# Attention and a two-layer network on one core: the second weights loaded ahead of two attention pairs, the second batch's pairs spread over more steps, and the leaky ReLU of twelve steps summed on GpSimd

## Chip, cores and metric

One Trainium2 chip, one core used. The metric is the device time of one execution in microseconds (us); several executions are made and their median is compared. The engines are TensorE (PE: matmuls; PEld: its weight loads), VectorE (DVE), ScalarE (ACT), GpSimd (POOL) and SyncE (SP), which issues the transfers (DMA).

## What is computed

q, k and v are 8 batches x 8 heads x 576 positions x 64, float32. Each head gets two attentions: a softmax over the sequence averaged down by 4 (144 positions), its result repeated 4 times, and a softmax over a band of |i - j| < 4. Their sum, laid out as 4608 tokens x 512, goes through two layers with a leaky ReLU between them. The layers' weights arrive as float64.

```
q_d, k_d, v_d = (a.reshape(B, H, 144, 4, 64).mean(axis=3) for a in (q, k, v))
out_up    = repeat(softmax(scale * q_d @ k_d.T) @ v_d, 4)
out_local = softmax(where(abs(i - j) < 4, scale * q @ k.T, -1e9)) @ v
x = (out_up + out_local) -> [4608, 512]
h = x @ w_in                                       # [4608, 2048]
g = maximum(h, 0.0) + alpha * minimum(h, 0.0)      # alpha: one per column of h
out = g @ w_out                                    # [4608, 512]
```

## The kernel before

**The stream.** The 4608 tokens are cut into 18 chunks of 256, the 2048 hidden columns into 8 pairs of 128; a *step* is one chunk and one pair, 144 steps in all, step 0 to 7 being the first chunk. Each float32 operand is split into an upper part (rounded to the type that TensorE multiplies at full speed) and a lower part, and each product is made of three: upper x upper, upper x lower, lower x upper. A step is: `hidden` (24 matmuls, L752, into PSUM tile h), `slopes` (ScalarE writes slope*h to tile t in SBUF and sign*h over h in PSUM, two halves each, L760 and L761), `larger` (VectorE takes the maximum of the two into t, L764), `split` (ScalarE rounds t to gh, L769; GpSimd subtracts, gl = t - gh, by the helper at L69) and `product` (24 matmuls, L798, into o). The sign belongs to the columns with alpha over 1; it is multiplied into the second layer's weights, so that a maximum serves for all.

**Weights.** Each pair's weights of w_in and w_out come as raw float64 (1 MB each, `load_raw`), as pairs of 32-bit words, and are turned into float32 parts by `make`: `magnitude` (ScalarE, L184, tile temp), `reach` (VectorE, L188 and L189), `bits` (VectorE, L193 and L194), `upper` (ScalarE: wih L199, or two halves of woh times sign, L203) and `lower` (VectorE: wil L207, or two halves of wol, L211). wih0, wil0 hold pairs 0 and 1, wih1 pairs 2 and 3, and so on. The first five pairs (`N_EARLY`) are decoded ahead of the stream, 128 x 1024 at a time; the last three beside steps 0 to 6 or so, by halves of 128 x 512, with their temporaries in PSUM (`bank`).

**The first batch** is computed ahead of the stream (`first_batch`), pair of heads by pair of heads: transfers of q, k (tile fqk) and v (fv), the averaging (L453, L455, L471, L473), scores, exponentials, the sums fxs (L512), and their split into xh (ScalarE, L518) and xl (VectorE, L519), the operands of hidden. The table `ORDER` lists in which order the one load queue (SyncE's) is given the transfers: `i0`..`i2` and `o0`..`o2` are raw weights of w_in and w_out of pair 0 to 2, `a0`..`a3` q, k and v of the four pairs of heads, `b0`..`b3` the windows of the local attention. For what stands before the stream the order on the other engines is left to a scheduler, which follows the priorities and the loads.

**The other batches** come in pieces beside the stream. For the averaged attention of pair hp of batch b, `down` makes: six loads (ld, L232), each with two folds on GpSimd (the helper `add`, L72; results s2q, s2k, s2v), `flip` (TensorE transposes, L250, tile qkT), `operands` (ScalarE copies qd and kd, L255 and L258), `scores` (TensorE, L263, tile s), `peak` (VectorE, L267), `exps` (ScalarE, L273 and L275, tile dp), `invert`, `scale` (ScalarE, L282), `turn` (TensorE transposes, L287, tile pT), `turned` (ScalarE copies, L291, tile th), `weigh` (TensorE, L297, tile pv) and `store`. The local attention of the later batches follows in units that begin at the times of the table `UNITS` and then every 5.92 steps.

**What sets the order.** From the stream on, all is written into a list of events, each with a time in *steps*; the program issues them sorted by it, and each engine executes its own in that order. hidden(s) stands at s - 1.95, slopes at s - 1.45, larger at s - 1.15, split at s - 1.0, product at s + 0.6. For `down`, the loads and folds begin at t0 (`FIRST[hp]` for batch 1), 0.4 steps apart, and the pieces behind them follow at t1 + pace * lag with the lags

```
(0, flip), (0.5, operands), (1.0, scores), (1.6, peak), (1.7, exps), (2.3, invert),
(2.4, scale), (3.0, turn, 0), (3.01, turn, 1), (3.4, turned, 0), (3.41, turned, 1),
(4.0, weigh), (4.5, store)
```

and t1 = t0 + 6 * gap + 0.3 (t1 = t0 for the first, whose folds are done in the start). pace is 0.75 for the four pairs of batch 1, 1.0 for all others. Pieces of batch 1 thus stand between steps 0 and 13.

## Time and profile before

| | us |
|---|---|
| median of 3 runs | 1014.43 |
| lowest to highest | 1014.23 to 1015.88 |
| the profiled execution's own time | 1012.62 |
| its span in the trace | 1010.8 |
| TensorE busy | 960.6 |
| VectorE busy | 832.8 |
| ScalarE busy | 560.2 |
| GpSimd busy | 482.1 |

The span goes from the first to the last instruction in the trace; the execution's own time has 1.8 us more around it. Busy time counts instructions in execution, not waits. The profile comes from one execution, the median from others.

### The profile page before, as it was taken

Reading aid. Unit: us, or ns where it says so; the run is one execution under the profiler, and the core shown is the slowest. Engines: PE = TensorE matmul, PEld = TensorE weight load, DVE = VectorE, ACT = ScalarE, POOL = GpSimd, SP = SyncE. Lnnn points to the kernel's source line nnn. Section 1 sums busy time; section 2 is a strip of 40 time slices with the busy share of each in tenths; the row PEclk is TensorE's granted clock in tenths of the full one; section 3 lists DMA queues with packets and bytes.
Section 4 is the critical chain, followed back from the end, with each engine's and each line's share of the span. In section 5 each row is a group of like instructions: output and inputs, shape, how many; then the busy total and the mean of one; then the engine's idle time right before and its main releaser. Section 6 shows DMA issues by size and latency. Waiting matters only on the chain.

```text
span 1010.8 us, 17864 instructions
## 1 busy us (share of the span) xinstructions
PE 960.6 (95%) x6402; PEld 852.7 (84%) x6402; DVE 832.8 (82%) x1347; ACT 560.2 (55%) x1483; POOL 482.1 (48%) x612
## 2 busy tenths in 40 slices
PE   5877989999999999999999999999999999999998
PEld 4756878898888898988888888888988898989997
DVE  6899988899888899899888898898898899997111
ACT  4767766465565555555455555555555554444442
POOL 2040645677665546555554544656555543323221
PEclk9856989999999999999999999999999999999999
DMA  8946443232422322433322332322331412210000
GB/s 191 222 148 242 123 153 98 83 119 83 145 83 73 118 81 78 121 97 93 103 88 66 100 111 71 125 80 74 123 100 60 131 49 61 86 43 22 1 21 22
DMA packets 61218, 98.26 MB, mean 97 GB/s; under 512 B 21578, under 2 KB 26954, under 8 KB 61130
## 3 DMA queue, kind: packets, MB, share of 16 engines
q1 hardware_dynamic: 60938, 96.87, 32.0%
q8 instruction: 50, 0.82, 0.3%
q10 hardware_dynamic: 192, 0.26, 0.1%
q14 instruction: 38, 0.31, 0.1%
HBM read 87.67 MB, written 9.44 MB: 96 GB/s over the span
## 4 chain that ended last, share of the span: by engine, by line
PE 72%; DVE 15%; ACT 4%; issue 3%; DMA 2%; POOL 2%; SPq 2%; DVEq 0%; ACTq 0%; POOLq 0%
PE o L798 33%; PE h L752 33%; DMA raw<-in_moe_w_out 2%; DVE qk L591 2%; DVE lb L650 2%; PE s L263 2%; DVE t L764 1%; PE pv L297 1%; DVE ls L595 1%; DVE temp L193 1%; DVE pv L647 1%; PE xp L659 1%; PE pT L287 1%; DVE temp L194 1%; DMA ld<-in_q 1%
## 5 line engine op out<-in xcount | busy, mean ns | idle before, releaser
L69 POOL TENSOR_TENSOR gl<-t,gh 128x512 fp32r<-128x512 f32 x144 | 186.5, 1295 | 390.8 <-ACT gh L769 347.4
L760 ACT ACTIVATE t<-h,slope 128x256 f32<-128x256 f32 x288 | 136.3, 473 | 203.0 <-PE h L752 166.2
L764 DVE TENSOR_TENSOR t<-h,t 128x512 f32<-128x512 f32 x144 | 99.0, 687 | 113.2 <-ACT h L761 108.6
L752 PE MATMUL h<-xh,wih 128*128 128x256 f32 x1152 | 190.9, 287 | 0.7 <-ACT xh L518 0.7
L798 PE MATMUL o<-woh,gh 128*128 128x512 f32 x576 | 188.1, 407 | 0.4 <-ACT woh L203 0.4
L752 PE MATMUL h<-xl,wih 128*128 128x256 f32 x1152 | 183.7, 281 | 0.6 <-POOL xl L69 0.6
L752 PE MATMUL h<-xh,wil 128*128 128x256 f32 x1152 | 184.1, 282 | 0.0
L798 PE MATMUL o<-wol,gh 128*128 128x512 f32 x576 | 182.1, 397 | 0.1
L798 PE MATMUL o<-woh,gl 128*128 128x512 f32 x576 | 182.1, 397 | 0.0
L752 PEld LDWEIGHTS h<-xh,wih 128*128 128x128 f32 x1152 | 163.5, 190 | 10.5 <-issue 1.8
L72 POOL TENSOR_TENSOR ld<-ld 72x256 f32<-72x256 f32 x168 | 125.4, 747 | 73.9 <-DMA ld<-in_q 49.4
L752 PEld LDWEIGHTS h<-xl,wih 128*128 128x128 f32 x1152 | 156.9, 190 | 0.8 <-POOL xl L69 0.8
L752 PEld LDWEIGHTS h<-xh,wil 128*128 128x128 f32 x1152 | 157.3, 190 | 0.0
L769 ACT CAST gh<-t 128x512 fp32r<-128x512 f32 x144 | 89.1, 619 | 118.7 <-DVE t L764 68.4
L595 DVE TENSOR_REDUCE ls<-qk 128x12 f32<-128x768 f32 (+1 forms) x126 | 136.4, 1083 | 2.8
L798 PEld LDWEIGHTS o<-woh,gl 128*128 128x128 f32 x576 | 108.6, 189 | 26.4
L798 PEld LDWEIGHTS o<-wol,gh 128*128 128x128 f32 x576 | 108.4, 188 | 26.4 <-DVE wol L211 0.7
L761 ACT ACTIVATE h<-h,sign 128x256 f32<-128x256 f32 x288 | 126.4, 439 | 0.0
L650 DVE TENSOR_TENSOR lb<-lb,pv 128x384 f32<-128x384 f32 x202 | 113.9, 564 | 5.5
L798 PEld LDWEIGHTS o<-woh,gh 128*128 128x128 f32 x576 | 98.3, 189 | 16.3 <-issue 2.2
L647 DVE TENSOR_TENSOR pv<-v,lb 128x1152 f32<-128x1152 f32 x84 | 93.6, 1115 | 2.6
L591 DVE TENSOR_TENSOR qk<-k,qp 128x768 f32<-128x768 f32 (+1 forms) x78 | 84.0, 1077 | 0.0
(148 smaller groups left out, 1111.4 us busy)
## 6 DMA issues: line engine op xcount, KB each, us to landing
k<-in_k SPq DMA_DIRECT2D x41, 384.0 KB
v<-in_v SPq DMA_DIRECT2D x41, 384.0 KB
raw<-in_moe_w_in SPq DMA_DIRECT2D x16, 512.0 KB
raw<-in_moe_w_out SPq DMA_DIRECT2D x16, 512.0 KB
ld<-in_q SPq DMA_DIRECT2D x56, 144.0 KB
ld<-in_k SPq DMA_DIRECT2D x56, 144.0 KB
ld<-in_v SPq DMA_DIRECT2D x56, 144.0 KB
q<-in_q SPq DMA_DIRECT2D x42, 192.0 KB
```

What stands on the lines that cost most here:

```text
L69: nc.gpsimd.tensor_tensor(o, a, b, op=ALU.subtract)
L72: nc.gpsimd.tensor_tensor(o, a, b, op=ALU.add)
L591: nc.vector.tensor_tensor(st["pr"][:, :nd], window(tiles[u, "k"], half, d0, nd), st["qp", half].unsqueeze(1).to_broadcast([128, nd, 2, 192 ...
L595: nc.vector.tensor_reduce(out=st["s"][:, half, d0:d0 + nd, :].rearrange("p a b -> p (a b)"), in_=st["pr"][:, :nd].rearrange("p a h (t d) - ...
L647: nc.vector.tensor_tensor(st["pr"][:, :nd], window4(tiles[u, "v"], half, d0, nd), prob(half, d0, nd), op=ALU.mult)
L650: nc.vector.tensor_tensor(st["acc"], st["acc"], st["pr"][:, i], op=ALU.add)
L752: nc.tensor.matmul(ph[:, j], w[:, m, 128 * o:128 * o + 128], x[:, m, :], start=(i == 0), stop=(i == 11))
L760: nc.scalar.activation(t[:, j], hs[st][:, j], AF.Copy, scale=slope[:, f:f + 1])
L761: nc.scalar.activation(hs[st][:, j], hs[st][:, j], AF.Copy, scale=sign[:, f:f + 1])
L764: nc.vector.tensor_tensor(gs[st], hs.pop(st), gs[st], op=ALU.max)
L769: nc.scalar.copy(gh, t)
L798: nc.tensor.matmul(outs[c][m], g[:, j, 128 * m:128 * m + 128], wo[w][n][:, o, :], start=(f == 0 and i == 0), stop=(f == NF - 1 and i == 2))
```

## The change

Four edits. `ORDER` moves i1 and o1 (the second raw weights) ahead of a2 and a3 respectively, with i2 ahead of b3. `down` runs batch 1's pairs at pace 1.0, and `FIRST` begins pair 2 at 2.8 and pair 3 at 5.3 steps. For steps 0 to 11 (`EARLY`) the leaky ReLU is written as a sum: slope*h + relu((sign - slope)*h), in which ScalarE writes the second term to a tile sh in SBUF and GpSimd adds it to t with the helper that does the folds; from step 12 on it stays a maximum on VectorE. One small subtraction makes gain = sign - slope.

```diff
--- before.py
+++ after.py
@@ -37,12 +37,13 @@
 FPT = ('ooo', 'ooo', 'ooo', 'oqo')
 FPV = ('ooo', 'ooo', 'ooo', 'qlq')
 EM = 'bbba'
-ORDER = 'i0 a0 a1 b0 o0 a2 b1 a3 b2 i1 b3 o1 i2'
+ORDER = 'i0 a0 a1 b0 o0 i1 a2 b1 o1 a3 b2 i2 b3'
 N_EARLY = 5
-FIRST = (-1.3, 0.3, 3.0, 5.7)
+FIRST = (-1.3, 0.3, 2.8, 5.3)
 T0_DEC, D_DEC = 0.5, 0.56
 UNITS = {3: 7.5, 4: 12.2, 5: 17.4, 6: 22.7, 7: 28.0}
 U_STEP = 5.92
+EARLY = 12
 BY_HALF = (5, 9, 13, 17, 21)
 FAR = {3: 2, 4: 2, 5: 2, 6: 2}
 
@@ -106,12 +107,14 @@
 
     sign = const.tile([128, NF], F32, name="sign")
     slope = const.tile([128, NF], F32, name="slope")
+    gain = const.tile([128, NF], F32, name="gain")
 
     def load_alpha():
         nc.sync.dma_start(slope, alpha.rearrange("(f p) -> p f", p=128))
         nc.vector.tensor_scalar(sign, slope, 1.0, 2.0, op0=ALU.is_le, op1=ALU.mult)
         nc.vector.tensor_scalar(sign, sign, -1.0, None, op0=ALU.add)
         nc.vector.tensor_tensor(slope, slope, sign, op=ALU.mult)
+        nc.vector.tensor_tensor(gain, sign, slope, op=ALU.subtract)
 
 
     wi, wo = ([[None] * 4, [None] * 4] for _ in range(2))
@@ -755,13 +758,24 @@
 
     def slopes(st):
         t = gs[st] = two.tile([128, 2, T], F32, tag="t", name=f"t{st}")
+        other = hs[st]
+        if st < EARLY:
+            other = late.tile([128, 512], F32, tag="xf", name=f"sh{st}").rearrange("p (j n) -> p j n", j=2)
         for j in range(2):
             f = 2 * (st % NP) + j
             nc.scalar.activation(t[:, j], hs[st][:, j], AF.Copy, scale=slope[:, f:f + 1])
-            nc.scalar.activation(hs[st][:, j], hs[st][:, j], AF.Copy, scale=sign[:, f:f + 1])
+            if st < EARLY:
+                nc.scalar.activation(other[:, j], hs[st][:, j], AF.Relu, scale=gain[:, f:f + 1])
+            else:
+                nc.scalar.activation(other[:, j], hs[st][:, j], AF.Copy, scale=sign[:, f:f + 1])
+        if st < EARLY:
+            hs[st] = other
 
     def larger(st):
-        nc.vector.tensor_tensor(gs[st], hs.pop(st), gs[st], op=ALU.max)
+        if st < EARLY:
+            add(gs[st], hs.pop(st), gs[st])
+        else:
+            nc.vector.tensor_tensor(gs[st], hs.pop(st), gs[st], op=ALU.max)
 
     def split(st):
         t = gs[st]
@@ -854,7 +868,7 @@
         def at(t, f, *args):
             events.append((t, len(events), f, args))
 
-        down(1, 0, FIRST[0], 0.0, 0.75, early=True)
+        down(1, 0, FIRST[0], 0.0, early=True)
     build_masks()
     late = ctx.enter_context(tc.tile_pool(name="late", bufs=1))
 
@@ -884,7 +898,7 @@
         b, hp = 1 + p // 4, p % 4
         if b == 1:
             if hp:
-                down(b, hp, FIRST[hp], 0.4, 0.75)
+                down(b, hp, FIRST[hp], 0.4)
     begin = dict(UNITS)
     for u in range(len(UNITS) + 3, 3 * B + 1):
         begin[u] = begin[u - 1] + U_STEP
```

In the changed kernel the same lines have numbers that are 1 to 14 higher: L72 becomes L73, L69 L70, L188 L191, L287 L290, L519 L522, L752 L755, L798 L812.

**VectorE, the last instructions ahead of the first chunk's last lower operand.** xl0 <- fxs30 belongs to the fourth pair of heads of the first batch; step 0 needs it. raw1_3 is w_out of the fourth pair of weights, raw0_4 w_in of the fifth. Before:

```order
L194 SCALAR_TENSOR_TENSOR temp_791<-raw0_3_847,temp_791 128x1024
L188 TENSOR_SCALAR temp_791<-temp_791 128x1024
L189 TENSOR_SCALAR temp_791<-temp_791 128x1024
L207 TENSOR_TENSOR wil1_830<-temp_791,wih1_829 128x4x256
L512 TENSOR_TENSOR fxs30_770<-fpv30_761,fod3_759 128x256
L193 SCALAR_TENSOR_TENSOR temp_791<-raw1_3_857,temp_791 128x1024
L512 TENSOR_TENSOR rest_89<-fpv38_787,fod3_759 128x64
L188 TENSOR_SCALAR temp_791<-temp_791 128x1024
L519 TENSOR_TENSOR xl0_313<-fxs30_770,xh0_312 128x256
```

With the change:

```order
L196 SCALAR_TENSOR_TENSOR temp_793<-raw1_3_859,temp_793 128x1024
L210 TENSOR_TENSOR wil1_832<-temp_793,wih1_831 128x4x256
L522 TENSOR_TENSOR xl1_330<-fxs24_633,xh1_329 128x256
L197 SCALAR_TENSOR_TENSOR temp_793<-raw1_3_859,temp_793 128x1024
L191 TENSOR_SCALAR temp_793<-temp_793 128x1024
L515 TENSOR_TENSOR fxs30_772<-fpv30_763,fod3_761 128x256
L192 TENSOR_SCALAR temp_793<-temp_793 128x1024
L214 SCALAR_TENSOR_TENSOR wol1_844<-temp_793,sign_78,woh1_843 128x512 x2
L515 TENSOR_TENSOR rest_91<-fpv38_789,fod3_761 128x64
L196 SCALAR_TENSOR_TENSOR temp_793<-raw0_4_871,temp_793 128x1024
L522 TENSOR_TENSOR xl0_315<-fxs30_772,xh0_314 128x256
```

The decoding has moved on ahead of xl0: the bit operations of raw1_3 and its lower parts (wol1) now stand before it, as does the first bit operation of raw0_4; counted from the program's start, two more bit operations of 128x1024, two more of wol's parts and one more scalar operation on temp stand ahead of it.

**GpSimd, from step 0 to the subtraction of step 2.** gl is the lower part of a step's g, t and sh are the two terms of the leaky ReLU, ld1_1 are the loads of the second pair of heads (pair 1) of batch 1 and s2q1_1 its folded q. Before:

```order
L69 TENSOR_TENSOR gl0_1008<-t0_995,gh0_1007 128x512
L69 TENSOR_TENSOR gl1_1066<-t1_1048,gh1_1065 128x512
L72 TENSOR_TENSOR ld1_1_0_1040<-ld1_1_0_1040 72x2x128
L72 TENSOR_TENSOR s2q1_1_1094<-ld1_1_0_1040 72x2x64
L72 TENSOR_TENSOR ld1_1_1_1046<-ld1_1_1_1046 72x2x128
L72 TENSOR_TENSOR s2q1_1_1094<-ld1_1_1_1046 72x2x64
L69 TENSOR_TENSOR gl2_1144<-t2_1107,gh2_1143 128x512
```

With the change:

```order
L73 TENSOR_TENSOR t0_997<-sh0_998,t0_997 128x512
L70 TENSOR_TENSOR gl0_1011<-t0_997,gh0_1010 128x512
L73 TENSOR_TENSOR t1_1047<-sh1_1048,t1_1047 128x512
L70 TENSOR_TENSOR gl1_1061<-t1_1047,gh1_1060 128x512
L73 TENSOR_TENSOR ld1_1_0_1039<-ld1_1_0_1039 72x2x128
L73 TENSOR_TENSOR s2q1_1_1089<-ld1_1_0_1039 72x2x64
L73 TENSOR_TENSOR ld1_1_1_1045<-ld1_1_1_1045 72x2x128
L73 TENSOR_TENSOR s2q1_1_1089<-ld1_1_1_1045 72x2x64
L73 TENSOR_TENSOR t2_1107<-sh2_1108,t2_1107 128x512
L70 TENSOR_TENSOR gl2_1138<-t2_1107,gh2_1137 128x512
```

Each step has an add ahead of its subtraction, and that of step 2 stands behind the folds of the two loads of q.

**TensorE, around hidden of step 7 (h7) and product of step 5 (o0 with gh5, gl5).** pT1_1 is the transposition of pair 1's probabilities dp1_1; qkT1_2 that of pair 2's folded q and k. Before:

```order
L752 MATMUL h7_1489<-xh0_312,wih3_1257 128x256 x4
L752 MATMUL h7_1489<-xh0_312,wil3_1258 128x256 x4
L752 MATMUL h7_1489<-xl0_313,wih3_1257 128x256 x4
L287 MATMUL pT1_1_0_1517<-ident_73,dp1_1_1438 72x96 x3
L287 MATMUL pT1_1_1_1521<-ident_73,dp1_1_1438 72x96 x3
L798 MATMUL o0_0_1112<-woh2_889,gh5_1399 128x512
L798 MATMUL o0_1_1113<-woh2_889,gh5_1399 128x512
```

With the change (the line of dots leaves out the rest of the product, of the same kind):

```order
L755 MATMUL h7_1496<-xl0_315,wih3_1259 128x256 x4
L253 MATMUL qkT1_2_1535<-ident_73,s2q1_2_1303 128x72 x2
L253 MATMUL qkT1_2_1535<-ident_73,s2k1_2_1377 128x72 x2
L812 MATMUL o0_0_1113<-woh2_891,gh5_1403 128x512
L812 MATMUL o0_1_1114<-woh2_891,gh5_1403 128x512
...
L812 MATMUL o0_1_1114<-woh2_891,gl5_1404 128x512
L290 MATMUL pT1_1_0_1577<-ident_73,dp1_1_1477 72x96 x3
L290 MATMUL pT1_1_1_1585<-ident_73,dp1_1_1477 72x96 x3
L755 MATMUL h8_1589<-xh1_329,wih0_81 128x256 x4
```

The transposition pT1_1 has moved from ahead of the product of step 5 to behind it, and the folds' transposition of pair 2 from behind the product to ahead of it.

## Rows read from the trace of the kernel before

**Rows 1.** The page: busy time of each engine, in us, share, instructions.
```profile
PE 960.6 (95%) x6402; PEld 852.7 (84%) x6402; DVE 832.8 (82%) x1347; ACT 560.2 (55%) x1483; POOL 482.1 (48%) x612
```

**Rows 2.** Windows: start:end, length; busy us (instructions) per engine; PEclk; DMA share; GB/s.
```profile
36.00:100.00 64.00, 49.30 (x376) 41.20 (x375) 62.77 (x103) 44.03 (x112) 15.07 (x13) 0.63 0.66 205
100.00:150.00 50.00, 45.38 (x276) 38.38 (x275) 43.15 (x69) 35.54 (x86) 27.55 (x39) 0.93 0.45 137
...
95.00:101.00 6.00, 6.00 (x35) 5.79 (x34) 5.17 (x7) 3.45 (x12) 0.69 (x1) 0.72 0.99 373
```

**Rows 3.** TensorE's timeline: start, duration (us), instructions; in brackets idle time before, releaser.
```profile
85.23 0.58 PE L752 MATMUL h<-xh,wih 128*128 128x256 f32 x1 [0.66 <-ACT xh L518]
...
94.65 1.34 PE L263 MATMUL s<-kd,qd 128*96 128x144 f32 x6 [2.13 <-ACT kd L258]
...
123.13 0.98 PE L263 MATMUL s<-kd,qd 128*96 128x144 f32 x6 [1.28 <-ACT kd L258]
...
134.04 1.14 PE L287 MATMUL pT<-ident,dp 96*72 96x96 f32 x6 [1.52 <-ACT dp L282]
...
141.21 0.34 PE L250 MATMUL qkT<-ident,s2q 72*128 72x72 f32 x2 [1.70 <-ACT th L291]
...
142.25 0.74 PE L752 MATMUL h<-xh,wih 128*128 128x256 f32 x4
...
146.73 0.90 PE L263 MATMUL s<-kd,qd 128*96 128x144 f32 x6
...
161.38 0.32 PE L250 MATMUL qkT<-ident,s2q 72*128 72x72 f32 x2 [0.99 <-POOL gl L69]
...
171.73 0.63 PE L752 MATMUL h<-xh,wih 128*128 128x256 f32 x4
...
174.53 0.63 PE L798 MATMUL o<-woh,gh 128*128 128x512 f32 x2
...
192.50 0.44 PE L659 MATMUL xp<-ident,x 128*128 128x128 f32 x2 [1.72 <-ACT kd L258]
```

**Rows 4.** Window inside the hidden part of step 8, columns as in rows 2.
```profile
144.00:146.00 2.00, 2.00 (x12) 2.00 (x11) 1.97 (x4) 1.25 (x4) 1.92 (x4) 0.50 0.00 0
```

**Rows 5.** VectorE's timeline, columns as in rows 3.
```profile
35.70 0.69 DVE L471 TENSOR_TENSOR fv<-fv 72x512 f32<-72x512 f32 x1 [2.62 <-DMA fv<-in_v]
...
85.81 0.41 DVE L519 TENSOR_TENSOR xl<-fxs,xh 128x256 fp32r<-128x256 f32 x1
86.15 1.22 DVE L194 SCALAR_TENSOR_TENSOR temp<-raw,temp 128x1024 int32<-128x1024 int32 x1
87.29 0.68 DVE L189 TENSOR_SCALAR temp<-temp 128x1024 int32<-128x1024 int32 x1
...
89.36 1.41 DVE L211 SCALAR_TENSOR_TENSOR wol<-temp,sign,woh 128x512 fp32r<-128x512 f32 x2
...
94.49 1.76 DVE L189 TENSOR_SCALAR temp<-temp 128x1024 int32<-128x1024 int32 x1
```

**Rows 6.** ScalarE's timeline.
```profile
99.98 1.32 ACT L203 ACTIVATE woh<-temp,sign 128x512 fp32r<-128x512 f32 x2
...
113.30 0.62 ACT L769 CAST gh<-t 128x512 fp32r<-128x512 f32 x1 [2.76 <-DVE t L764]
```

**Rows 7.** Groups by line: busy us, mean ns, idle before and its main releaser.
```profile
L69 POOL TENSOR_TENSOR gl<-t,gh 128x512 fp32r<-128x512 f32 x144 | 186.5, 1295 | 390.8 <-ACT gh L769 347.4
...
L764 DVE TENSOR_TENSOR t<-h,t 128x512 f32<-128x512 f32 x144 | 99.0, 687 | 113.2 <-ACT h L761 108.6
...
L761 ACT ACTIVATE h<-h,sign 128x256 f32<-128x256 f32 x288 | 126.4, 439 | 0.0
```

**Rows 8.** GpSimd's timeline.
```profile
93.91 1.78 POOL L69 TENSOR_TENSOR gl<-t,gh 128x512 fp32r<-128x512 f32 x1 [31.63 <-ACT gh L769]
...
104.05 0.74 POOL L72 TENSOR_TENSOR ld<-ld 72x256 f32<-72x256 f32 x1 [0.77 <-DMA ld<-in_q]
...
106.64 1.29 POOL L69 TENSOR_TENSOR gl<-t,gh 128x512 fp32r<-128x512 f32 x1
```

## The prediction

> **What bounds the kernel now.** I read the page first. TensorE is busy 95% of the span, VectorE 82%, ScalarE 55%, GpSimd 48% [rows 1]. From about 200 us on TensorE hardly stops, and the change touches nothing there but an offset, so the question is how early the two-layer stream reaches, say, step 12, and what it loses on the way.
>
> The windows come next [rows 2]. From 36 to 100 us VectorE is busy 62.8 of 64 us while TensorE runs at a mean granted clock of 0.63: there VectorE sets the pace. It works off the first batch's attention and the decoding of the weights in one fixed order. From 100 to 150 us VectorE is still busy 43.2 of 50 us and TensorE 45.4, at a clock of 0.93.
>
> Then TensorE's timeline [rows 3]. The first step's matmuls start to run in earnest at 85.23 us. After that TensorE executes a fixed order of steps with small pieces of the second batch's pairs between them, and each time it stops, a piece stands at the head of the queue: 2.13, 1.28, 1.52, 1.70 and 0.99 us, and 1.72 us at 192.50, each waiting for ScalarE or GpSimd, which wait for VectorE or each other. Of the five that end from 94.65 us (first scores) to 161.38 us, ahead of the hidden part of step 12 at 171.73 us, the last four make 5.5 us (the 1.28 us one, of scores too, ends at 123.13 us). Two stretches run at half clock as well: the hidden part of step 8, inside which the granted clock is 0.50, the lower of its two levels (1.2 of 2.4 GHz) [rows 4], takes 146.73 - 142.25 = 4.48 us, where that of step 12 takes 174.53 - 171.73 = 2.80 us [rows 3], so 1.7 us is lost; and the product ahead of it loses about as much (from 134.04 us to 141.21 less the wait of 1.70 are 5.47 us, of which the piece at the front has 1.14 less some 0.2 of overlap: 4.5 us, against 2.8). In all some 8.9 us of the stream can be won back: 5.5 idle and 3.4 at half clock.
>
> **The change, part by part.**
>
> *Loads.* The second weights' two transfers move ahead of the third and fourth pair's q, k, v on the one load queue. For the start this matters through VectorE's order, which the scheduler rewrote with it. I counted what stands ahead of the first chunk's last low operand (xl0 of the fourth pair, at 85.81 us [rows 5]) on VectorE in both programs. The attention work is the same; the changed order has two more of the 1024-wide bit operations, two more 512-wide lower parts and one more 1024-wide scalar operation. Durations from start to next start: 87.29 - 86.15 = 1.14 us; the pair of lower parts 1.32 us, the row's 1.41 less the overlap of some 0.08 that the row before shows (1.22 against 1.14); 0.60 us for the scalar operation, the row's 0.68 less the same [rows 5]. Sum 2 x 1.14 + 1.32 + 0.60 = 4.2 us more work ahead of the stream.
>
> Against that, VectorE waited 2.62 us at 35.70 us for the fourth pair's v [rows 5]. In the changed order 15 more instructions stand ahead of that one, 8 to 9 us of work by the same durations, whereas its data are pushed back by 2 MB. At the window's 205 GB/s 2 MB is 10.2 us; at the 373 GB/s of 95 to 101 us, in which weights land, it is 5.6 [rows 2]. That leaves a wait between 0 and 4.3 us; these 2 MB are weights, so I take the fast end: the wait about vanishes. Handshakes with ScalarE now stand elsewhere (the second weights' magnitude is ahead of the exponentials of pair 1 on ScalarE), and I charge 0.6 us for them. Start: 4.2 - 2.6 + 0.6 = **+2.2 us**. Bounds: +1.6 (wait gone, nothing new) and +6 (wait stays, as much again new).
>
> Behind xl0, ScalarE now has the two signed upper parts of the fifth output weights ahead of the first gh and of the pair's q and k copies, 1.32 us for the two [rows 6], and they wait for VectorE's last bit operation. VectorE needs 6.8 us from the start of xl0 to the end of that (three bit operations, one lower part, two scalar operations and three short ones at the durations above), then ScalarE about 2.7: the first scores start 9.6 us after xl0 instead of 94.65 - 85.81 = 8.8. That is another **+0.8 us**; bounds 0 and +1.5.
>
> *The leaky ReLU.* Twelve max operations of 687 ns leave VectorE and twelve adds appear on GpSimd; the only add of that shape and engine in the trace is the subtraction of 1295 ns [rows 7]. ScalarE has as many instructions as before; a Relu with a scale to SBUF is not in the trace, and I take the 439 ns of the line that it replaces [rows 7]. So VectorE gets 12 x 0.6 = 7.2 us freer between 92 and 176 us, and the chain of one step becomes 0.6 us longer. A step's chain has room: between hidden(s) and product(s) TensorE runs two products and two hidden parts, four times 2.8, 11.2 us.
>
> The adds wait in GpSimd's in-order queue. In the second order piece the add of step 2 stands behind the folds of the first two loads of pair 1, which wait for their transfers. Before, the first fold starts at 104.05 us, having waited 0.77 us for its transfer, and the two loads take until 106.64 [rows 8]. In the code these transfers are issued behind the last raw weights, into room that the start's last operand releases. That moves with the start, so the folds end near 109 us and the add near 110. ScalarE is through with the exponentials at 99.98 before [rows 6], 3 us later now, and has four parts of the leaky ReLU and a magnitude left, 2.3 us, ahead of gh of step 2: from about 105.5 it stands still for some 4 to 5 us. Behind it are queued the decoding's upper parts, the scaling that pT of pair 0 waits for, and the next step's slopes; VectorE waits for the upper parts. TensorE itself feels about 1 us. Before, ScalarE had the same kind of wait on VectorE's max (2.76 us at 113.30 [rows 6]).
>
> A rule of the Trainium skill speaks against this part: "SBUF — State Buffer", section "Who interferes with whom", says that VectorE and GpSimd share a port pair, that a VectorE operation with two SBUF inputs or in a two-port mode and a GpSimd operation exclude each other, and that the second waits the whole of the first. The trace has such a case: a scalar operation that takes 0.68 us took 1.76 at 94.49, beside a GpSimd subtraction that took 1.78 instead of 1.295 [rows 5, 8]. By the row a collision costs 1.1 us. But from step 2 on the decoding's temporaries lie in PSUM and their rows beside GpSimd work are not stretched, so I charge it for the first add only (within the +0.8); if the rule hit every add it would be 12 x 1.1 = 13 us of VectorE time.
>
> *Pace.* The first pairs' pieces are spread over a third more steps. In the PE piece of the order pT of pair 1 moves behind product 5, and all pieces that made TensorE stop get 2.8 to 5.6 us more of cover, against waits of 1 to 1.7 us. Their inputs come no later, save for what GpSimd adds. I keep 3.9 us of the 8.9 as lost: 0.9 at pT of pair 0 (the scaling behind gh of step 2), 1.3 in short waits near steps 6 to 8, where decoding and adds meet, and one stretch at half clock, 1.7. Stream: **-5.0 us**. Bounds: 0 and -8.9.
>
> *Behind step 12* both programs issue the same. VectorE is ahead of TensorE by about 1 us more than before, so of the 1.72 us at 192.50 I take off half: **-0.9 us**; bounds 0 and -1.7.
>
> Sum: +2.2 + 0.8 - 5.0 - 0.9 = -2.9 us. The profiled execution has 1010.8 us of span and 1.8 us around it, 1012.6; the median of the runs is 1.8 above that, 1014.43. So 1009.7 for a profiled one, and **1011.5 us** as a median.
>
> **Rivals.**
>
> 1. *GpSimd becomes the wait that VectorE was* (no change). gh of each of steps 2 to 7 waits for an add behind folds that wait for transfers, ScalarE stands still 2 to 5 us each time, VectorE behind it, and the waits of [rows 3] return at other pieces. For: the folds waited for transfers already at 104.05. Against: later folds mostly find their data. Stream gain 2.5, half of mine: +3.0 - 2.5 - 0.4, about 1014.5.
>
> 2. *The stream just starts later* (slower). VectorE does 4.2 us more first, and no wait goes: with the 0.8 that is +5, and TensorE keeps its waits since ScalarE, not VectorE, holds the pieces; gain 2, so +3 and 1017.4. It decides if the first long run of step 0 begins later than about 89.5 us (85.23 + 4.2). For it speaks that VectorE has no idle time from 36 to 100 us that could absorb it [rows 2].
>
> 3. *All stalls go* (faster). The pieces have cover, VectorE is 10% lighter per step, no half clock. +2.2 - 8.9 - 1.7 = -8.4: 1006. Against it: the wait at gh of step 2.
>
> 4. *Every add collides with VectorE*: 13 us on an engine that sets the pace until step 8 or so; half of it reaches the end: +6.5 on the no-change case, 1020. By the page of the Trainium skill named above this would be the rule; the rows from 104 us on don't show it.
>
> **How the numbers follow.** Mine 0.38 (1008 to 1012.4), rival 1 0.27, rival 2 0.18, rival 3 0.14, rival 4 0.03. A measurement of this kernel can tell about 0.2%, 2 us, from no change. Faster: 0.38 + 0.14 = 0.52; same 0.27; slower 0.18 + 0.03 = 0.21. The range leaves out the outer half of rival 3 and rival 4 with the outer part of rival 2: 1006.5 to 1017. My own case alone is 1008 to 1013.
>
> **What would show it.** Right, step by step: the wait for v of the fourth pair is under 1 us; xl0 of that pair starts at 87 to 89 us; the first scores at 97 to 98.5; a ScalarE wait of 3 us or more for GpSimd at gh of step 2; TensorE waits between the first scores and step 12 under 4 us with at most one stretch at half clock; hidden of step 12 at 169 to 171 us, and the shift there carried to the end. Wrong: xl0 beyond 90 us, ScalarE's waits for GpSimd above 10 us in the twelve steps, VectorE rows stretched to 1.7 us beside adds, or a wait behind step 14 that was not there.

## The result, and the profile after

The changed kernel was slower: 1017.97 us median of 19 runs (1015.41 to 1024.16), against 1015.26 us of 19 runs before (1010.22 to 1021.73). The ratio is 1.0036, 95% interval 1.0021 to 1.0051, or about 3.7 us (0.0036 x 1015.26; the two medians lie 2.7 us apart). The forecast was 1011.5 us, faster, with a range of 1006.5 to 1017: the time lies outside it.

Single executions of one kernel lie up to 8.8 us (changed) and 11.5 us (before) apart, so a profile is one draw. The profiled execution of the changed kernel took 1015.64 us, its span is 1013.6 us, 2.8 us more than before. I account for that span first and then ask what the other runs say.

The page gives the busy time of each engine:

```profile
PE 961.5 (95%) x6402; PEld 853.5 (84%) x6402; DVE 825.1 (81%) x1336; ACT 561.0 (55%) x1483; POOL 496.7 (49%) x624
```

Against [rows 1] VectorE has lost 7.7 us and GpSimd has won 14.6 us, as foreseen; TensorE is as busy as before. Four windows (busy us and instructions of PE, PEld, DVE, ACT, POOL; then granted clock, DMA share, GB/s):

```profile
36.00:100.00 64.00, 48.86 (x365) 40.62 (x364) 58.94 (x100) 43.99 (x114) 18.16 (x16) 0.71 0.60 190
100.00:150.00 50.00, 42.09 (x263) 35.70 (x261) 37.49 (x59) 32.63 (x82) 35.47 (x46) 0.93 0.44 135
260.00:264.00 4.00, 3.08 (x10) 2.53 (x11) 3.69 (x5) 1.68 (x5) 0.38 (x1) 0.66 0.30 100
531.00:534.00 3.00, 3.00 (x16) 3.00 (x15) 2.28 (x4) 0.41 (x2) 2.28 (x5) 0.50 0.55 178
```

The first two answer to [rows 2]. From 100 to 150 us VectorE is 5.7 us less busy, and so is TensorE, by 3.3 us: VectorE was relieved and TensorE stood still more. The last two lie where before had a clock of 1.00 (260 to 264 and 530 to 533 us of its trace); 0.50 is the lower of TensorE's two levels (1.2 of 2.4 GHz).

TensorE's timeline, the rows that answer to [rows 3]:

```profile
84.92 0.58 PE L755 MATMUL h<-xl,wih 128*128 128x256 f32 x1 [0.72 <-DVE xl L522]
...
94.35 0.98 PE L266 MATMUL s<-kd,qd 128*96 128x144 f32 x6 [1.92 <-ACT kd L261]
...
107.70 1.14 PE L290 MATMUL pT<-ident,dp 96*72 96x96 f32 x6 [1.14 <-ACT dp L285]
...
135.95 0.89 PE L290 MATMUL pT<-ident,dp 96*72 96x96 f32 x3 [1.55 <-ACT dp L285]
141.51 0.70 PE L290 MATMUL pT<-ident,dp 96*72 96x96 f32 x3 [4.67 <-ACT kd L261]
141.91 1.20 PE L755 MATMUL h<-xh,wih 128*128 128x256 f32 x4
...
146.98 0.72 PE L812 MATMUL o<-woh,gh 128*128 128x512 f32 x2
...
170.85 0.63 PE L755 MATMUL h<-xh,wih 128*128 128x256 f32 x4
```

The first chunk's last operand arrives at 84.92 us, the first scores run at 94.35 (94.65 before). The rows show one large wait: the second of two transpositions of pair 1, alone at 141.51 us, after 4.67 us, with ScalarE's kd named as what ended it. Product 6 starts at 146.98 (147.37 before), hidden of step 12 at 170.85 (171.73). So the stream is 0.9 us ahead there, and it stays so up to this:

```profile
191.58 0.44 PE L662 MATMUL xp<-ident,x 128*128 128x128 f32 x2 [1.69 <-ACT kd L261]
...
260.92 0.45 PE L290 MATMUL pT<-ident,dp 96*72 96x96 f32 x3 [1.88 <-ACT th L294]
261.15 1.06 PE L812 MATMUL o<-woh,gh 128*128 128x512 f32 x2
```

```profile
530.52 0.41 PE L290 MATMUL pT<-ident,dp 96*72 96x96 f32 x3 [2.50 <-DVE lb L619]
530.72 1.00 PE L755 MATMUL h<-xh,wih 128*128 128x256 f32 x4
...
535.15 0.62 PE L812 MATMUL o<-woh,gh 128*128 128x512 f32 x2
```

The rows of the kernel before at the same place as the last three:

```profile
529.32 0.41 PE L287 MATMUL pT<-ident,dp 96*72 96x96 f32 x3 [2.49 <-DVE lb L616]
529.51 0.72 PE L752 MATMUL h<-xh,wih 128*128 128x256 f32 x4
```

Behind a wait of 1.88 us the product runs with 1.06 us for two matmuls (0.63 to 0.70 at full clock), and behind a wait of 2.50 us hidden of step 67 takes 535.15 - 530.72 = 4.43 us; before, a wait of 2.49 us stands there without such a loss. Laying product on product of both traces, the changed kernel falls back by 1.54 us between products 23 and 24 and by 1.55 us at product 65, and by nothing else above 0.5 us from step 12 to the end. From -0.9 us at step 12 it goes to -0.4 at product 23 (that wait is 0.4 us longer than before's), +1.1, and +2.8 at the end. In this profile, then, the whole loss arises behind step 12.

VectorE, ScalarE and GpSimd of the changed kernel, the rows for [rows 5], [rows 6] and [rows 8]:

```profile
40.03 0.68 DVE L474 TENSOR_TENSOR fv<-fv 72x512 f32<-72x512 f32 x1
...
84.44 0.42 DVE L522 TENSOR_TENSOR xl<-fxs,xh 128x256 fp32r<-128x256 f32 x1
...
92.20 1.89 DVE L214 SCALAR_TENSOR_TENSOR wol<-temp,sign,woh 128x512 fp32r<-128x512 f32 x2 [0.79 <-ACT woh L206]
...
99.10 0.70 DVE L192 TENSOR_SCALAR temp<-temp 128x512 int32<-128x512 int32 x1
```

```profile
101.01 0.64 ACT L187 ACTIVATE temp<-raw 128x512 f32<-128x512 f32 x1
106.23 0.62 ACT L783 CAST gh<-t 128x512 fp32r<-128x512 f32 x1 [4.58 <-POOL t L73]
...
140.06 0.62 ACT L783 CAST gh<-t 128x512 fp32r<-128x512 f32 x1 [1.02 <-POOL t L73]
140.59 0.58 ACT L258 ACTIVATE qd<-qkT 64x144 f32<-64x144 f32 x2
141.18 0.28 ACT L261 COPY kd<-qkT 128x144 f32<-128x144 f32 x1
```

```profile
93.60 1.60 POOL L70 TENSOR_TENSOR gl<-t,gh 128x512 fp32r<-128x512 f32 x1 [0.73 <-ACT gh L783]
...
102.46 0.74 POOL L73 TENSOR_TENSOR ld<-ld 72x256 f32<-72x256 f32 x1 [3.29 <-DMA ld<-in_q]
...
104.91 1.29 POOL L73 TENSOR_TENSOR t<-sh,t 128x512 f32<-128x512 f32 x1
...
133.09 1.29 POOL L73 TENSOR_TENSOR t<-sh,t 128x512 f32<-128x512 f32 x1
```

VectorE takes up the fourth pair's v at 40.03 us without a wait and xl0 at 84.44 us. ScalarE stands 4.58 us at gh of step 2 for GpSimd's add, which runs at 104.91 us behind folds whose transfer was waited for 3.29 us. At 140.06 us gh of step 7 waits for an add too, and the copies qd and kd of pair 2 come behind it: TensorE's transposition begins 0.05 us after kd ends.

### The profile page after: what moved, and what is told of

It is laid out like the page before. It is cut to its first block, busy times and chain, and to the rows that moved or that the text cites. A ratio compares the mean times of both kernels' runs of the same rounds, so it can differ in the third digit from the quotient of the medians.

```text
span 1013.6 us, 17844 instructions
## 1 busy us (share of the span) xinstructions
PE 961.5 (95%) x6402; PEld 853.5 (84%) x6402; DVE 825.1 (81%) x1336; ACT 561.0 (55%) x1483; POOL 496.7 (49%) x624
## 4 chain that ended last, share of the span: by engine, by line
PE 76%; DVE 12%; ACT 4%; POOL 3%; issue 2%; SPq 2%; DMA 1%; DVEq 0%; ACTq 0%; POOLq 0%
PE h L755 34%; PE o L812 34%; PE s L266 2%; DVE lb L653 1%; PE pv L300 1%; DVE qk L594 1%; DVE ls L598 1%; PE pT L290 1%; PE xp L662 1%; DVE t L778 1%; PE fs L448 1%; ACT t L766 1%; DVE pv L650 1%; POOL t L73 1%; DVE temp L196 1%
## 5 line engine op out<-in xcount | busy, mean ns | idle before, releaser
L70 POOL TENSOR_TENSOR gl<-t,gh 128x512 fp32r<-128x512 f32 x144 | 186.3, 1294 | 336.0 <-ACT gh L783 291.8
L755 PE MATMUL h<-xh,wih 128*128 128x256 f32 x1152 | 191.6, 288 | 0.5 <-ACT xh L521 0.2
L812 PE MATMUL o<-woh,gh 128*128 128x512 f32 x576 | 188.4, 408 | 0.0
L778 DVE TENSOR_TENSOR t<-h,t 128x512 f32<-128x512 f32 x132 | 90.8, 688 | 116.8 <-ACT h L770 112.3
L755 PE MATMUL h<-xl,wih 128*128 128x256 f32 x1152 | 184.7, 282 | 1.4 <-DVE xl L522 0.7
L755 PE MATMUL h<-xh,wil 128*128 128x256 f32 x1152 | 184.7, 282 | 0.0
L812 PE MATMUL o<-wol,gh 128*128 128x512 f32 x576 | 182.1, 397 | 0.4 <-DVE wol L214 0.4
L812 PE MATMUL o<-woh,gl 128*128 128x512 f32 x576 | 181.7, 396 | 0.0
L755 PEld LDWEIGHTS h<-xh,wih 128*128 128x128 f32 x1152 | 163.9, 191 | 10.3 <-issue 1.8
L73 POOL TENSOR_TENSOR ld<-ld 72x256 f32<-72x256 f32 x168 | 127.6, 760 | 72.9 <-DMA ld<-in_q 47.5
L755 PEld LDWEIGHTS h<-xl,wih 128*128 128x128 f32 x1152 | 157.5, 190 | 1.9 <-DVE xl L522 1.0
L755 PEld LDWEIGHTS h<-xh,wil 128*128 128x128 f32 x1152 | 157.9, 191 | 0.0
L812 PEld LDWEIGHTS o<-wol,gh 128*128 128x128 f32 x576 | 108.6, 189 | 26.9 <-DVE wol L214 0.9
L812 PEld LDWEIGHTS o<-woh,gl 128*128 128x128 f32 x576 | 108.5, 188 | 26.4
L770 ACT ACTIVATE h<-h,sign 128x256 f32<-128x256 f32 x264 | 116.2, 440 | 0.0
L812 PEld LDWEIGHTS o<-woh,gh 128*128 128x128 f32 x576 | 98.5, 189 | 15.6 <-issue 2.2
```

Of the source, the lines that this page charges most:

```text
L70: nc.gpsimd.tensor_tensor(o, a, b, op=ALU.subtract)
L73: nc.gpsimd.tensor_tensor(o, a, b, op=ALU.add)
L755: nc.tensor.matmul(ph[:, j], w[:, m, 128 * o:128 * o + 128], x[:, m, :], start=(i == 0), stop=(i == 11))
L770: nc.scalar.activation(other[:, j], hs[st][:, j], AF.Copy, scale=sign[:, f:f + 1])
L778: nc.vector.tensor_tensor(gs[st], hs.pop(st), gs[st], op=ALU.max)
L812: nc.tensor.matmul(outs[c][m], g[:, j, 128 * m:128 * m + 128], wo[w][n][:, o, :], start=(f == 0 and i == 0), stop=(f == NF - 1 and i == 2))
```

## Experiments

Each was executed 10 to 12 times (e11 6 times) beside the kernel before. The rows of the table stand in the order in which they are compared below, not in that of the runs.

| run | what is changed against before | ratio to before (95%) | span of its profile |
|---|---|---|---|
| e1 | load order | 1.0012 (0.9994 to 1.0031) | 1011.5 |
| e2 | pace and FIRST | 0.9994 (0.9977 to 1.0010) | 1011.6 |
| e3 | sum, 12 steps | 1.0015 (0.9997 to 1.0034) | 1017.7 |
| e4 | order, sum | 1.0032 (1.0014 to 1.0051) | 1016.0 |
| e12 | pace, sum | 0.9993 (0.9972 to 1.0014) | 1008.9 |
| the change | order, pace, sum | 1.0036 (1.0021 to 1.0051) | 1013.6 |
| e5 | the change, copies at lag 0.4 | 0.9999 (0.9982 to 1.0016) | 1010.8 |
| e10 | the change, copies at lag 0.04 | 1.0005 (0.9989 to 1.0022) | 1012.2 |
| e6 | pace, copies at lag 0.4 | 0.9987 (0.9969 to 1.0004) | 1009.6 |
| e9 | pace, copies at lag 0.04 | 0.9966 (0.9948 to 0.9983) | 1009.8 |
| e7 | order, sum for 6 steps | 1.0002 (0.9983 to 1.0021) | 1010.5 |
| e11 | pace, sum for 6 steps, lag 0.04 | 0.9944 (0.9926 to 0.9963) | 1006.5 |
| e8 | one memset more on VectorE | 1.0004 (0.9985 to 1.0023) | 1015.3 |

**First theories.** A: the 4.67 us wait and the two half-clock stretches are the loss. B: GpSimd's adds hold ScalarE and that is the loss. C: the loads make the start later, as I had predicted.

**e1, the load order alone.**

```diff
-ORDER = 'i0 a0 a1 b0 o0 a2 b1 a3 b2 i1 b3 o1 i2'
+ORDER = 'i0 a0 a1 b0 o0 i1 a2 b1 o1 a3 b2 i2 b3'
```

> Only the load order of the change; pace, FIRST and the maximum on VectorE stay as before. Theory A (the start is not dearer, the loss lies where pair 2's folded transposition takes the PSUM buffer that pair 1's second transposition needs, and in later half-clock stretches): the fourth pair's xl0 starts at 84 to 85 us as in the changed kernel (85.81 before), the order of TensorE beside the stream is the old one, so there is no wait above 2 us near step 6; the product of step 0 starts 1 to 2 us earlier than before and the run is 0 to 2 us faster. Theory B (GpSimd's adds are the loss): the same start, also no loss. Theory C (the loads are the loss, the recorded prediction's +2.2 and +0.8): xl0 at 87 to 89 us and the run 2 to 3 us slower.

xl0 of the fourth pair started at 87.75 us, the first scores at 97.41, product 0 2.7 us later than before; by product 12 only 0.6 us of that was left, and 0.7 at the end. A's start was wrong: with VectorE's start order the same as the changed kernel's but for the one small instruction for gain, xl0 came 3.3 us later. The start of the changed kernel's profile had been a lucky draw. C's start came true (87 to 89 us), but its 2 to 3 us of time are neither shown nor excluded: the interval of 1.0012 goes from 0.9994 to 1.0031.

**e2, the pace alone.**

```diff
-FIRST = (-1.3, 0.3, 3.0, 5.7)
+FIRST = (-1.3, 0.3, 2.8, 5.3)
-        down(1, 0, FIRST[0], 0.0, 0.75, early=True)
+        down(1, 0, FIRST[0], 0.0, early=True)
-                down(b, hp, FIRST[hp], 0.4, 0.75)
+                down(b, hp, FIRST[hp], 0.4)
```

> Only the pace and FIRST of the change; loads and maximum as before. Theory A: the second transposition of pair 1 again stands in TensorE's order behind pair 2's folded transposition and waits for its copy on ScalarE, 2 to 5 us of wait at one place between the products of steps 5 and 6, and 0.5 to 1 us at the same place of pairs 2 and 3; the run is 1 to 4 us slower than before. Theory B: without the adds gh of step 7 comes early enough, that wait is under 1 us and the run is 0 to 3 us faster. Theory C: no loss here, 0 to 3 us faster.

TensorE's timeline of e2 at the two transpositions of pair 1:

```profile
136.38 0.89 PE L287 MATMUL pT<-ident,dp 96*72 96x96 f32 x3 [0.65 <-ACT dp L282]
141.75 0.69 PE L287 MATMUL pT<-ident,dp 96*72 96x96 f32 x3 [4.49 <-ACT kd L258]
```

The wait is there without a single add on GpSimd, 4.49 us, so B's account of it falls. A's price falls too, for the run is within 0.2% of before: from product 0 to product 5 the pace had won 2.3 us (0.99 to 3.31 us ahead of before), and product 6 lost 3.4 again.

**e3, the sum alone** (the change without the load order, pace and FIRST).

> Only the twelve steps' sum on GpSimd; loads, pace and FIRST as before. Theory A: ScalarE waits for GpSimd's add at gh of step 2 for 2 to 5 us, but TensorE has no wait above 2 us in the first twelve steps, and the run is within 1.5 us of before. Theory B: TensorE loses 3 us or more between the first scores and step 12, and the run is 2 to 4 us slower. Theory C: within 1.5 us.

ScalarE's wait at gh of step 2 is 2.32 us, but TensorE waits 2.59 us at 142.65 and 2.83 us at 165.13 us, the latter for GpSimd's gl, with half clock behind it; at 534.63 us it waits 2.50 us, again with half clock behind. A said no wait above 2 us and was wrong; the time, +1.5 us, lies at A's edge and short of B's 2 to 4.

**e4, order and sum** (the change without pace and FIRST).

> The change without its pace and FIRST, so the pairs of batch 1 do not overlap in the two PSUM buffers. Theory A: the 4.67 us wait at pair 1's second transposition is gone, step 12 is reached 3 to 5 us earlier than in the changed kernel, and the run is 2 to 5 us faster than before. Theory B: GpSimd's adds still hold ScalarE, the run is as slow as the changed kernel, +2 to +4 us. Theory C: slower than before by 2 us or more.

A falls as the whole explanation: without the overlap this was as slow as the whole change, as B and C said. TensorE of e4 (x2: two matmuls; a product is 12 of them in six such rows, not 24):

```profile
163.57 0.32 PE L253 MATMUL qkT<-ident,s2q 72*128 72x72 f32 x2 [2.81 <-POOL gl L70]
...
163.81 0.92 PE L812 MATMUL o<-woh,gh 128*128 128x512 f32 x2
164.53 1.06 PE L812 MATMUL o<-wol,gh 128*128 128x512 f32 x2
...
168.33 0.71 PE L300 MATMUL pv<-th,s2v 72*64 72x144 f32 x8
```

TensorE waits 2.81 us for GpSimd ahead of the product of step 8, and the product behind it takes 168.33 - 163.81 = 4.5 us. So the sum has a cost of its own at the old pace, in its later steps. That made the next theory: (1) the pace wins in steps 0 to 5 and loses it to the overlap; (2) the sum in steps 6 to 11 costs at the old pace; (3) the loads cost a little.

**e5, the change with pair 2's copies ahead of gh of step 7.** In `down`:

```diff
-        for lag, f, *args in ((0, flip), (0.5, operands),
+        for lag, f, *args in ((0, flip), (0.4 if b == 1 else 0.5, operands),
```

> The changed kernel with one move: for batch 1 ScalarE's copies of the folded transposition (qd, kd) stand at lag 0.4 instead of 0.5, so that those of pair 2 come ahead of gh of step 7 on ScalarE instead of behind it. Theory A (two pairs overlap in the two PSUM buffers; pair 1's second transposition waits for pair 2's copy): the 4.67 us wait before hidden of step 8 falls under 1.5 us, the product of step 6 starts 3 to 4 us earlier relative to the product of step 5 than in the changed kernel, and the run is 2 to 4 us faster than the changed kernel, so within 1.5 us of before. Theory B (ScalarE is held by GpSimd's adds, whatever stands behind): the wait only moves to another piece, the product of step 6 starts within 1 us of its place in the changed kernel, no gain.

ScalarE, then TensorE of e5:

```profile
139.06 0.58 ACT L258 ACTIVATE qd<-qkT 64x144 f32<-64x144 f32 x2
139.65 0.28 ACT L261 COPY kd<-qkT 128x144 f32<-128x144 f32 x1
139.83 0.64 ACT L187 ACTIVATE temp<-raw 128x512 f32<-128x512 f32 x1
140.73 0.62 ACT L783 CAST gh<-t 128x512 fp32r<-128x512 f32 x1 [0.26 <-POOL t L73]
```

```profile
136.60 0.89 PE L290 MATMUL pT<-ident,dp 96*72 96x96 f32 x3 [1.43 <-ACT dp L285]
139.99 0.70 PE L290 MATMUL pT<-ident,dp 96*72 96x96 f32 x3 [2.49 <-ACT kd L261]
...
146.25 0.72 PE L812 MATMUL o<-woh,gh 128*128 128x512 f32 x2
```

kd now runs at 139.65 us, ahead of gh at 140.73, and the transposition starts 0.06 us after it ends; its wait is 2.49 us. From product 5 to product 6 e5 falls back against the kernel before by 2.42 us instead of 3.92: 1.5 us won, not 3 to 4, since the copies stand behind the leaky ReLU's instructions of step 7. But the run is 0.37% faster than the changed kernel, and the two intervals do not meet: (1) holds in the change. In the profile 1.55 us of the gain is the half-clock stretch near 261 us, which is absent, with a wait of 1.46 us there.

**e6, the pace alone with the same move.**

> Loads and maximum as before, pace and FIRST of the change, and the same move of the copies ahead of gh of step 7. Theory A: the pace alone had won 2.3 us by the product of step 5 and lost 3.4 us at that of step 6 by the 4.49 us wait; without that wait the product of step 6 starts 2 to 4 us earlier than before, and the run is 1.5 to 4 us faster than before. Theory B: without adds on GpSimd there was nothing to hold ScalarE, the wait was due to something else and stays at 3 us or more, time as with the pace alone, within 1 us of before.

The wait is 2.60 us; product 6 is 1.49 us ahead of before (e2: 0.07 behind), short of A's 2 to 4. 0.9987 is in the direction expected and not certain; against e2 the move is worth 0.07%, within the noise.

**e7, order and sum, with `EARLY = 6`.**

> The loads' order and the sum, the sum for steps 0 to 5 only; pace and FIRST as before. Theory A (GpSimd's adds in steps 6 to 11 delay the folds, on which pair 3's folded transposition waits 2.81 us for GpSimd near 163 us, and half-clock matmuls follow): that wait is back at about 1 us and the stretch of 1.5 us behind it is gone, so the run is 2 to 4 us faster than with twelve steps' sum and the loads' order, near before plus 0 to 1.5. Theory B (it is the wait at gh of step 2 that costs): no change, 3 us slower than before.

TensorE at the place of e4's wait:

```profile
160.97 0.32 PE L253 MATMUL qkT<-ident,s2q 72*128 72x72 f32 x2 [0.99 <-POOL gl L70]
...
161.21 0.71 PE L812 MATMUL o<-woh,gh 128*128 128x512 f32 x2
...
164.19 0.71 PE L300 MATMUL pv<-th,s2v 72*64 72x144 f32 x8
```

As expected: 0.99 us of wait, and the product takes 2.98 us at full clock. The ratio goes from 1.0032 to 1.0002, although gh of step 2 still waits 3.92 us for GpSimd. The two intervals still overlap a little; the traces decide it: from product 7 to product 9 e3 and e4 both fall back against before by 2.5 us, e7 by nothing. (2) holds; the wait at gh of step 2, the one I had priced, is not what costs.

**e8, one memset more.** A const tile spot, 128x64, and

```diff
+    at(64.86, nc.vector.memset, spot, 0.0)
```

> The kernel before with one more instruction on VectorE, a memset of 128x64, behind the maximum that runs at 526.5 us, in the chain for which TensorE waits 2.49 us at 529 us. In the traces with a wait of 2.44 to 2.49 us there the clock stayed at 1.00, in the three with 2.50 us the next matmuls ran at 0.50 and 1.5 us was lost. Theory A (the wait's length decides): the wait is 2.55 to 2.7 us, half-clock matmuls follow, and what comes later is 1.5 to 1.8 us later than before relative to the product ahead of it. Theory B (chance, or something in the sum): the clock stays at 1.00 and 0.1 to 0.2 us is lost.

```profile
530.98 0.67 PE L288 MATMUL pT<-ident,dp 96*72 96x96 f32 x3 [2.54 <-DVE lb L617]
531.35 1.20 PE L753 MATMUL h<-xh,wih 128*128 128x256 f32 x4
...
536.62 0.88 PE L799 MATMUL o<-woh,gh 128*128 128x512 f32 x2
```

The wait grew to 2.54 us and hidden of step 67 ran for 536.62 - 531.35 = 5.27 us. That looked like A, but what came later undid it (below).

**e9 and e10, copies at once.** The lag of `operands` is 0.04 for batch 1 in the pace alone (e9) and in the whole change (e10).

> Loads and maximum as before, pace and FIRST of the change, and batch 1's copies of the folded transposition at lag 0.04, right behind it, so ahead of the leaky ReLU's instructions of step 7 too. Theory A (pair 1's second transposition waits for the buffer that pair 2's copy frees): the wait of 2.60 us with the copies at lag 0.4 falls under 1 us, the product of step 6 starts 1 to 3 us earlier relative to that of step 5, and the run is 2 to 5 us faster than before. Theory B (the copy is not what is waited for, ScalarE's scaling of the probabilities is): the wait moves to the first transposition and nothing is won, 1 us faster than before as with lag 0.4.

> The changed kernel, whole, with batch 1's copies at lag 0.04. Theory A: the wait of 4.67 us (2.49 at lag 0.4) falls under 1 us; stream as with the pace alone; 0.5 to 1.5 us slower than the pace with the copies at once, since twelve adds on GpSimd win nothing and the start comes half a us later; 0 to 3 us faster than before. Theory B: GpSimd's adds hold ScalarE at gh of steps 2 and 6, so the run is not faster than before.

TensorE of e9:

```profile
134.08 0.74 PE L798 MATMUL o<-woh,gh 128*128 128x512 f32 x2 [1.72 <-ACT woh L203]
135.58 1.22 PE L798 MATMUL o<-wol,gh 128*128 128x512 f32 x2 [0.77 <-DVE wol L211]
...
139.39 0.70 PE L287 MATMUL pT<-ident,dp 96*72 96x96 f32 x3 [0.96 <-ACT kd L258]
```

The second transposition waits 0.96 us, under 1 us as A said, but 1.72 and 0.77 us now stand ahead of it, for upper and lower parts of the weights: in this profile product 6 gains nothing over e6 (1.66 us ahead of before), as B said, while the runs are 3.5 us faster than before, as A said. Other kernel, other draws: the profile does not show where the runs won. In e10 the wait is 1.06 us and the time is within 0.2% of before and 0.4% over e9, so B's, not A's; gh of step 2 waits 5.79 us for GpSimd there and pT of pair 0 4.42 us for ScalarE, so with the copies at once this wait does reach TensorE.

**e11, pace, `EARLY = 6`, copies at once, old load order.**

> Loads as before, pace and FIRST of the change, copies at lag 0.04, and the sum on GpSimd for steps 0 to 5 only. Theory A: as the pace with the copies at once, within 1 us of it, 2 to 5 us faster than before; the wait at gh of step 2 for GpSimd is 2 to 5 us and costs TensorE under 1 us. Theory B (the adds that meet folds waiting for transfers cost): 1 us or more slower than without the sum.

The best, 1009.4 us median of 6 runs, 0.56% under before. That is more than A's 2 to 5 us, but the interval meets e9's. gh of step 2 waits 2.57 us, as said, but TensorE feels more than the 1 us of A: it waits 3.93 us for ScalarE at pT of pair 0. Its xl0 at 83.14 us is the earliest of all traces. Why this kernel is the fastest is not shown.

**e12, the change with the old load order.**

> The changed kernel with the old load order: pace, FIRST and the twelve steps' sum only. If the parts add up (order alone 1.0012 of before, sum alone 1.0015, pace alone 0.9994, order and sum 1.0032, the whole change 1.0036), this one is 1.5 to 2.5 us slower than before and the load order is worth about 1 us of loss in the whole. If the whole loss needs the start of the new order (rival: late start), it is within 0.8 us of before. The wait at pair 1's second transposition is 4 us or more in either case, and ScalarE's wait at gh of step 2 for GpSimd is 2 to 5 us.

0.9993: not the 1.5 to 2.5 us slower, but what the rival of the late start said. Multiplied, the single edits give 1.0009 for pace and sum and 1.0021 for all three, both still inside the measured intervals, so it is not shown that the parts don't add up. At the new pace no cost of the sum is seen (e2: 0.9994), and the load order makes the difference of 0.43% to the whole change. The wait at pair 1's second transposition is 4.68 us; that at gh of step 2 is 1.64 us, not 2 to 5.

## Why the prediction was wrong

**Where the miss lies.** Forecast were -2.9 us, measured +3.7, a miss of 6.6. e12, the change without the load order, splits it. Pace, sum and what follows behind step 12 were to bring -5.0 - 0.9 = -5.9 us and brought -0.7 (0.9993): 5.2 us of the miss. The load order was to cost 2.2 + 0.8 = 3.0 us and costs 4.4 (0.43%): the other 1.4. By e12's interval each share is known to about 2 us.

**What bounds the kernel: right in part.** Up to step 12 the terms are the right ones. But what comes behind is more than an offset: in the profile step 12 is 0.9 us ahead and the end 2.8 us behind.

**Start, +2.2 us, and first scores, +0.8.** The wait for v went, as said. In the profile xl0 came 1.4 us earlier instead of 2.2 later, so on this trace the step failed. Over all fourteen traces it is the size that was off: with the new load order xl0 started at 84.44, 85.98, 86.45, 86.84, 87.17 and 87.75 us (mean 86.4), with the old one at 83.14, 83.83, 85.53, 85.56, 85.81, 85.95, 86.73 and 86.93 (mean 85.4): +1.0 us, and a spread of 3 to 4 us with nearly the same instructions. From xl0 to the first scores it took 94.35 - 84.44 = 9.9 us, against 9.6 forecast. The order's cost in runs is larger than that: 0.12% (e1), 0.17% (e4 over e3) and 0.43% (the change over e12), on average 2.4 us. In the whole change that is shown (the intervals of e12 and of the change don't meet). How 1.0 us of start becomes 2.4 or more is shown only in part. The record of the executions, divided after the fact, has this: in the six kernels with the new order 22 of 79 executions have a mean granted clock of 0.981 to 0.989 and take 3.1 to 6.0 us longer than the other executions of the same kernel (by medians), whose clock is 0.976 or less; of the 186 with the old order whose clock is on record 2 reach 0.981, one of them the fastest of its kernel. Without them e1 is no slower than before (1014.51 against 1014.84 us), while the change is still 2.2 us slower. No trace was taken of such an execution, so what happens in it stays open.

**The leaky ReLU.** The wait of 4 to 5 us at gh of step 2 was 4.58, about 4 us earlier than forecast, and TensorE felt 1.14 us of it at 107.70 us: the mechanism is right, the size in part luck, since it is 3.88 to 5.79 us in the five traces with sum and new order and 1.64 to 2.57 in the three with sum and old order. What I missed is the other end of the twelve steps: at the old pace the adds of steps 6 to 11 make TensorE wait 2.81 us for GpSimd ahead of product 8 and lose 1.5 us more at half clock (e4 against e7: 0.30%). At the new pace that wait does not occur, and no cost of the sum is seen (e12 against e2). A collision of VectorE and GpSimd shows at the first step: the two lower parts at 92.20 us took 1.89 us (1.41 in [rows 5]), with a subtraction of 1.60 at 93.60 (1.295 in [rows 7]). From 98 us on the decoding's rows are about 0.70 us long, like that at 99.10, and adds 1.29, like those at 104.91 and 133.09. The rule of the Trainium skill ("SBUF — State Buffer", "Who interferes with whom"), that of two such operations one waits while the other holds the shared ports, thus shows at 0.5 us here, and of the twelve steps on the first only; rival 4 fell.

**Pace, -5.0 us: the step that failed.** From the first scores to hidden of step 12 the changed kernel needs 170.85 - 94.35 = 76.5 us, the kernel before 171.73 - 94.65 = 77.1: 0.6 us won instead of 5.0. The runs of the pace alone say as much (e2: 0.9994). TensorE's waits in that stretch, forecast at under 4 us, add up to 8.5 (1.14, 0.43, 1.55, 4.67 and 0.68), against 5.9 before. That hidden of step 12 still came within the forecast 169 to 171 us was luck: the early start of this trace made up for the gain that was not there.

"All pieces that made TensorE stop get 2.8 to 5.6 us more of cover" and "their inputs come no later" looked at what a piece reads and not at where it writes. The pieces live in two PSUM buffers (`bank("d")`). At pace 0.75 pair 1's copies out of them (lag 3.41, so at step 3.0 + 2.56) end ahead of pair 2's folded transposition at 5.7; at pace 1.0 they stand at 6.4 and pair 2 begins at 5.5. Two pairs then share two buffers, and pair 1's second transposition waits until pair 2's copy, which stands behind gh of step 7 on ScalarE, has freed one. The order piece in front shows it: qkT1_2 had moved ahead of the product of step 5 and pT1_1 behind it. I read there only that pT1_1 had cover.

From the first scores to product 5 the changed kernel needs 130.65 - 94.35 = 36.3 us against 134.96 - 94.65 = 40.3, 4.0 us won; at product 6 it has lost 3.9 of them. Not all of that is the buffer: 1.5 us go when the copy is moved (e5), and 2.2 to 2.6 us stay in e5, e6 and e9 alike. pT1_1 with its wait now stands behind product 5 instead of ahead of it (1.52 us of wait and 1.14 of work in [rows 3]), so a part of the 4.0 us was no gain but an exchange. e2 shows that the pace makes the wait; e5, e6 and e9 show that the copy's place sets its length (4.67 to 2.49, 4.49 to 2.60 and 0.96 us). In runs the move is worth 0.37% in the change; with the pace alone it is worth 0.07% at lag 0.4, within the noise, and 0.28% at lag 0.04.

**Behind step 12, -0.9 us.** In the profile it was +3.6. The wait at 192.50 us was 1.69 us (at 191.58) instead of 1.72: nothing won. And I left the clock out: half-clock stretches of 1.54 and 1.55 us at two places where before had a wait and no loss, and 0.4 us more of wait at the first of them.

**Rivals.** Rival 2 (later, slower, 1017.4) had the time by another road: the start was a part, no wait "kept by ScalarE" but a new one. Rival 1 (GpSimd becomes the wait) is what the sum alone does at the old pace. No rival named a buffer.

## What to carry to other kernels

When pieces of independent work are spread over more time, compare how long each now holds its buffers with the distance to the next one; if holding time is over the distance, the in-order engines make one piece wait for the other's release, and the release may stand behind an unrelated wait. Move the copy that frees the buffer right behind the work that filled it before judging a schedule: here that turned +0.36% into 0 and, with the loads left as they were and half of the sum, into -0.56% (six runs). And with runs spread over 10 us, a gain or loss of 3 us needs both many runs and a trace laid step by step against the other one.

## What the hardware showed beyond that

The half-clock stretch behind the wait near 530 us came in 8 of 14 traces and cost about 1.5 us (e8: 2.6). I first took the wait's length for the cause: 2.44 to 2.49 us without, 2.50 to 2.54 with it, in the first ten traces. e9 then had it with 2.45 us, e11 with 2.48, e10 not with 2.50, and e12 not with 2.52:

```profile
527.44 0.41 PE L290 MATMUL pT<-ident,dp 96*72 96x96 f32 x3 [2.52 <-DVE lb L619]
527.63 0.71 PE L755 MATMUL h<-xh,wih 128*128 128x256 f32 x4
...
530.51 0.64 PE L812 MATMUL o<-woh,gh 128*128 128x512 f32 x2
```

Hidden of step 67 takes 530.51 - 527.63 = 2.88 us here. So the length does not decide, and which execution is hit stays open. Near 261 us it came in three of four traces with a wait of 1.88 us and in none of ten with 1.46 to 1.50; the wait of 1.88 us occurs only at the new pace, in four of its eight traces. One such stretch more or less is 0.15% of the time, as much as most of the edits here.
